# Padded rows for the split down weights, and later free times in the list of TensorE's work

## Chip, core and metric

The kernel runs as one program on 1 core of a Trainium2 chip. The metric is the device time of one execution in microseconds (us). TensorE (PE) multiplies, VectorE (DVE), ScalarE (ACT) and GpSimd (POOL) work on what it leaves in PSUM, and SyncE (SP) issues most DMAs.

## What is computed

```python
xn = layernorm(x)                      # x: 1 x 2048 x 576, float32
q, k, v = split(xn @ wqkv)             # 32 heads of 18 columns
p = softmax(q @ k.T * 18 ** -0.5)      # per head, 2048 x 2048
s = heads(p @ v) @ wo
g = silu(((xn @ w_gate) * (xn @ w_up)) @ w_down)   # 4608 inner columns, no bias
return x + s * g
```

All operands are float32. The kernel keeps the accuracy by splitting each operand into a high part (rounded to the format that TensorE reads at one pass) and a low part (the rest), and sums three products of parts.

## The kernel before

**Stages.** A first part (to about 193 us) normalizes x, makes the columns of x, q, k and v, and splits weights. A middle part computes the 32 heads and the whole gated feed-forward together. A last part (from about 2501 us) multiplies by wo and by the gate.

**Two halves of the array.** In the middle part nearly all matmuls use 64 rows of the array, and two run at once, one on each half (row 0 and row 64). PE takes its instructions in one queue, in the order in which the program lists them. That order is worked out while the program is built, by `order()`: it keeps a clock for each half (`clk[0]`, `clk[1]`), always serves the half that is behind, and picks an item whose inputs and PSUM bank it counts as free. Nothing of this runs on the chip: there only the order remains, and semaphores hold an instruction back where the order was too early.

**The items.** Scores for the row maxima (`a_item`, L712, bank `pa`, read by DVE, L714); scores for the exponentials (`b_item`, L764, bank `pb`, read by ACT, L766); gate and up columns (`gu_op`, L815, 27 matmuls of 512 columns in one of four banks `pg`); down (`down_op`, L876, passes of 6 matmuls of 288 columns). A down pass does six on half 0, hands its bank over to half 1 through a semaphore instruction on another engine (`handing`), and does six on half 1 into the same bank. There are 72 units (4 chunks of 512 tokens by 18 pairs of 128 inner columns), each with 8 such passes. A product of the exponentials with v (`pv_group`, L775, called by `visit`) uses the whole array for up to 8 tiles of a head: three visits for each of the first three heads, two for each other one, 67 in all for 512 tiles. `small` and `soon_now` put the work of the other engines into the same list.

**What the list counts.** An item of 512 columns costs `WIDE` 0.2267 us of its half, one of 288 columns `SHORT` 0.1315 us. `engine(eng, start, length)` gives the end of an operation of another engine; the engine is counted as taken for `length - HIDDEN[eng]` only. A bank counts as free `SPARE` (banks a and b) or `SPARE_G` (the four banks of `pg`) after the end of the operation that reads it, and a handed-over bank a fixed time after the end of the semaphore instruction (`handed`):

```python
HIDDEN = {"DVE": 0.085, "ACT": 0.11, "POOL": 0.03}
SPARE, SPARE_G = 0.27, 0.20
banks[tag][slot] = engine("DVE", clk[r] + 0.43, 0.685) + SPARE
handed[n, k // 6] = engine(eng, clk[0] + 0.33, 0.06) + 0.16
```

**Down's weights.** For each unit the tile `wd` (one buffer) holds, in each of 128 partitions, `[j][e][576]` numbers: j of two blocks of 128 inner columns, e high or low part, and 576 output columns, which are read as two halves of 288 (i = 0, 1). A row of 576 takes 2,304 B, so the second half starts 1,152 B behind the first. In the first pass over the 18 column pairs they are split on the chip (`d_get`: ACT L294, POOL L295) and stored to DRAM (`swd`, L302); the 50 later loads (L286) fetch them from there, as does the last one (`wdl`, L236). `d_get` for the next unit is called when the unit's last down pass has been issued, and the load is queued on SP.

**Raw weights of the first part.** `w_load` fetches blocks of wqkv into one of two buffers of the tag `wraw` (L111, L114); `w_split` reads them (ACT L129, POOL L133). The same tag later holds raw gate and up columns (`g_raw`) and sums (`acc2`).

Of the kernel before, what the change touches and what calls it, by code (L numbers as in the profile page):

```python
# [20 lines left out]
FT = mybir.dt.float32  # L21
# [3 lines left out]
OP = mybir.AluOpType  # L25
# [16 lines left out]
def kernel(  # L42
# [36 lines left out]
    sg = dram.tile([S, D], FT, name="sg")  # L79
    swo = dram.tile([128, 10, D], FT, name="swo")  # L80

    turns = [0]

    def bank(tag, bufs, k=None):
        if tag == "g":
# [20 lines left out]

    def w_load(srcs):

        raw = wpool.tile([128, 2, 5, 128], FT, name="wraw", bufs=2)[:, 0:len(srcs)]
        for i, (m, c0) in enumerate(srcs):  # L110
            nc.sync.dma_start(raw[:, i, 0:4, :],  # L111
                              m[0:512, c0:c0 + 128].rearrange("(k p) c -> p k c", p=128))
            for b in (0, 64):
                nc.sync.dma_start(raw[b:b + 64, i, 4, :], m[512:576, c0:c0 + 128])  # L114
        return raw
# [41 lines left out]
        return wpool.tile([128, 18, 128], FR, name="wgu", bufs=2)  # L157

    def d_tile():
        return wpool.tile([128, 2, 2, D], FR, name="wd", bufs=1)  # L160

    chores, later = [], []
    soon, moves, ordering = [], [], []
    HIDDEN = {"DVE": 0.085, "ACT": 0.11, "POOL": 0.03}
    clk, free, split_at = [0.0, 0.0], {"DVE": 0.0, "ACT": 0.0, "POOL": 0.0}, {}

    def chore(all=True):
# [50 lines left out]
    def columns_of(u):  # L220
        c, q = units[u]
        return NF2 - 1 - q if c % 2 else q
# [8 lines left out]
    def g_get(n):  # L231

        if n == 2 * len(units):
            u = n // 2 - 1
            dw[u] = wpool.tile([128, 2, 2, D], FR, name="wdl", tag="wgu", bufs=2)
            nc.sync.dma_start(dw[u].bitcast(FT), swd[columns_of(u)])  # L236
            ddone.add(u)
        if n >= 2 * len(units):
            return
        f = 2 * columns_of(n // 2) + n % 2  # L240
        if n > 1 and n // 2 % NF2 == 0:
            gw[n] = gw[n - 2]
            gdone.add(n)
            return
        w = gw[n] = g_tile()
        if n >= 2 * NF2:
            nc.sync.dma_start(w.bitcast(FT), swg[f])
            gdone.add(n)
            return
        if n not in graw:  # L250
            ready(gdone, n - 2)
            moves_now()
        raw = graw.pop(n)

        def piece(b):
            nc.scalar.activation(w[:, b:b + 3, :], raw[:, b:b + 3, :], AF.Copy)  # L256
            nc.gpsimd.tensor_tensor(w[:, 9 + b:12 + b, :], raw[:, b:b + 3, :], w[:, b:b + 3, :].bitcast(FT),  # L257
                                    op=OP.subtract)

        def end():  # L260
            gdone.add(n)
            split_at["g", n] = free["POOL"] + 0.2

            def keep():
                nc.sync.dma_start(swg[f], w.bitcast(FT))
                g_load(n + 2)

            move(free["POOL"], keep)

        chores.extend([(piece, (b,)) for b in (0, 3, 6)] + [(end, ())])  # L270
# [5 lines left out]
    def d_get(n):  # L276
        if n >= len(units) - 1:
            return
        p = columns_of(n)
        if n and n % NF2 == 0:  # L280
            dw[n] = dw[n - 1]
            ddone.add(n)
            return
        w = dw[n] = d_tile()
        if n >= NF2:
            nc.sync.dma_start(w.bitcast(FT), swd[p])  # L286
            ddone.add(n)
            return
        if n not in draw:
            moves_now()  # L290
        raw = draw.pop(n)

        def big_piece(k):
            nc.scalar.activation(w[:, k, 0, :], raw[:, k], AF.Copy)  # L294
            nc.gpsimd.tensor_tensor(w[:, k, 1, :], raw[:, k], w[:, k, 0, :].bitcast(FT), op=OP.subtract)  # L295

        def end():
            ddone.add(n)
            split_at["d", n] = free["POOL"] + 0.2

            def keep():
                nc.sync.dma_start(swd[p], w.bitcast(FT))  # L302
                d_load(n + 1)

            move(free["POOL"], keep)

        chores.extend([(big_piece, (k,)) for k in range(2)] + [(end, ())])
# [385 lines left out]
    with ExitStack() as mid:  # L693
# [179 lines left out]
        def down_op(r, u, s, i, ps, n, by):  # L873
            own = alone(u, 2 * s + i)
            j, a, e = DTERMS[n]
            op = nc.tensor.matmul(ps[:, 0:HALF], hs[u][half[r], j, a, s * 128:(s + 1) * 128],  # L876
                             dw[u][half[r], j, e, i * HALF:(i + 1) * HALF],
                             start=(own or r == 0) and n == 0, stop=(own or r == 1) and n == len(DTERMS) - 1)
            if not own and r == 0 and n == len(DTERMS) - 1:
                handing[u, s, i] = by.nop()  # L880
                after(handing[u, s, i], op)
            if not own and r == 1 and n == 0:
                after(op, handing.pop((u, s, i)))
# [202 lines left out]
        slots, gone = {}, [0.0, 0.0]  # L1086
        banks = {"a": [0.0] * 2, "b": [0.0] * 2, "g": [0.0] * 4}
        turn = {"a": 0, "b": 0}
        SPARE, SPARE_G = 0.27, 0.20

        def next_free(tag):
            if tag == "g":
# [236 lines left out]
        def order():  # L1329
# [5 lines left out]
            while going(0) or going(1) or na < TOTAL or nb < TOTAL or due or jobs or soon or pool_later:  # L1335
# [33 lines left out]
                elif op is not None:  # L1369
# [10 lines left out]
                        handed.pop((n, k // 6), None)  # L1380
                    own = kind == "d" and alone(n, k // 6)
                    if kind == "d" and r == 0 and k % 6 == 5 and not own:
                        handed[n, k // 6] = engine(eng, clk[0] + 0.33, 0.06) + 0.16
                        kept[n, k // 6] = slots[0, kind]
                    if end:
                        if kind == "d":
# [136 lines left out]
```

## Time and profile before

| what | value |
|---|---|
| median of 3 runs | 2568.65 us (2568.43 to 2568.83) |
| the profiled execution | 2568.51 us |
| its span, first to last instruction | 2566.7 us |
| PE matmul busy in the span | 2556.5 us |
| DVE, ACT, POOL busy | 1801.8, 1550.5, 682.4 us |
| granted clock of TensorE | 1.00 of full speed |
| DMA queues, time of their packets | 55% of 16 engines' span |

Matmuls are pipelined: the record of one begins before that of its forerunner on the same half has ended, so the engine can read as busy throughout and still lose time. What one costs is the distance from its start to the start of the next on the same half. A row of the timeline joins instructions of one kind that follow each other, and gives the start of the first, the time to the end of the last, and their number; brackets give the idle time of the engine before it, and what ended it.

### The profile page before, as it was taken

The page shows a single profiled execution, that of the slowest core. Times are in us where ns is not written, and L with a number is a line of the kernel's source. Part 1 is how long each engine was busy: PE and PEld are TensorE (multiplying, and loading weights), DVE is VectorE, ACT ScalarE, POOL GpSimd, SP SyncE. Part 2 cuts the span into 40 slices and gives each one's busy share as a digit, 9 for nine tenths or more (in the row PEclk, how much of TensorE's full clock was granted, in tenths as well). Part 3 has the DMA queues.
Part 4 walks back from the last instruction along what each step waited for, and adds up shares of the span by engine and source line. Part 5 has one row for each costly group of instructions (what it writes and reads, how often), then busy time and mean ns, then how long its engine had stood idle before and what let it go on. Part 6 is the DMA issues. An engine that isn't in the chain of part 4 may idle for free.

```text
span 2566.7 us, 59619 instructions
## 1 busy us (share of the span) xinstructions
PE 2556.5 (100%) x24439; PEld 2109.0 (82%) x24439; DVE 1801.8 (70%) x2995; ACT 1550.5 (60%) x3093; POOL 682.4 (27%) x705
## 2 busy tenths in 40 slices
PE   9999999999999999999999999999999999999999
PEld 8899877887887888877788878888788788877789
DVE  6208777777777777777677777777777777777438
ACT  4223677666766656665666656766665666666532
POOL 3214444434421222121211112222211222222016
PEclk9999999999999999999999999999999999999999
DMA  7899767676654345455454445443453453433348
GB/s 234 264 299 261 206 179 193 190 201 193 181 181 136 134 161 159 147 156 166 156 178 130 141 140 165 138 137 137 142 164 107 165 169 129 144 130 125 122 161 268
DMA packets 186641, 435.65 MB, mean 170 GB/s; under 512 B 51104, under 2 KB 112192, under 8 KB 156160
## 3 DMA queue, kind: packets, MB, share of 16 engines
q1 hardware_dynamic: 184208, 423.88, 53.6%
q0 software_dynamic: 2160, 7.96, 0.8%
q8 instruction: 192, 3.15, 0.5%
q14 instruction: 81, 0.66, 0.1%
HBM read 315.16 MB, written 111.35 MB: 166 GB/s over the span
## 4 chain that ended last, share of the span: by engine, by line
PE 98%; DVE 1%; ACT 0%; DMA 0%; issue 0%; SPq 0%; ACTq 0%; DVEq 0%
PE pg L815 36%; PE pg L775 18%; PE pg L876 16%; PE pa L712 11%; PE pb L764 8%; PE pb L493 2%; PE pa L493 2%; PE pg L556 2%; PE pg L1472 1%; PE pa L1472 1%; PE pb L1472 1%; DMA xin<-in_A_x_dram 0%; PE pg L402 0%; PE pa L764 0%; DVE mx L714 0%; PE pb L712 0%
## 5 line engine op out<-in xcount | busy, mean ns | idle before, releaser
L714 DVE TENSOR_REDUCE mx<-pa 128x1 f32<-128x512 f32 x2016 | 1337.3, 686 | 344.9 <-PE pb L764 158.6
L766 ACT ACTIVATE pt<-pb 128x512 f32<-128x512 f32 x2007 | 1149.5, 602 | 478.7 <-PE pb L764 390.5
L815 PE MATMUL pg<-xc,wgu 64*128 64x512 f32 x7776 | 1370.1, 388 | 0.0
L815 PEld LDWEIGHTS pg<-xc,wgu 64*128 64x128 f32 x7776 | 1034.7, 184 | 50.1
L876 PE MATMUL pg<-wd,hs 64*128 64x288 f32 x6816 | 843.2, 293 | 0.0
L876 PEld LDWEIGHTS pg<-wd,hs 64*128 64x128 f32 x6816 | 784.4, 184 | 11.1 <-issue 0.8
L712 PE MATMUL pa<-whole,turning 64*128 64x512 f32 x1999 | 773.7, 394 | 0.5 <-DVE mx L714 0.3
L764 PE MATMUL pb<-whole,turning 64*128 64x512 f32 x1984 | 769.1, 394 | 0.5 <-ACT pt L766 0.3
L775 PE MATMUL pg<-pt,vt 128*32 128x512 f32 x4096 | 453.4, 594 | 0.0
L856 POOL TENSOR_TENSOR hs<-us,hs 128x512 fp32r<-128x512 f32 x144 | 185.8, 1290 | 922.0 <-ACT hs L840 696.8
L712 PEld LDWEIGHTS pa<-whole,turning 64*128 64x128 f32 x1999 | 362.9, 184 | 69.5 <-issue 53.8
L764 PEld LDWEIGHTS pb<-whole,turning 64*128 64x128 f32 x1984 | 360.2, 184 | 6.8 <-ACT pt L766 1.2
L775 PEld LDWEIGHTS pg<-pt,vt 128*32 128x32 f32 x4096 | 126.3, 110 | 284.8 <-issue 280.7
L903 POOL TENSOR_TENSOR acc<-acc,st 128x288 f32<-128x288 f32 x285 | 230.0, 809 | 486.7 <-ACT st L933 303.3
L781 DVE TENSOR_TENSOR oc<-oc,pg 128x512 f32<-128x512 f32 x35 | 24.1, 688 | 219.9 <-PE pg L775 206.4
L257 POOL TENSOR_TENSOR wgu<-wraw,wgu 128x384 fp32r<-128x384 f32 x108 | 108.3, 1016 | 211.7 <-ACT wgu L256 139.9
L779 ACT ACTIVATE oc<-pg 128x512 f32<-128x512 f32 x32 | 19.1, 598 | 229.0 <-PE pg L775 211.1
L939 DVE TENSOR_TENSOR acc<-acc,pg 128x288 f32<-128x288 f32 x260 | 116.0, 448 | 32.5 <-PE pg L876 28.4
L933 ACT ACTIVATE st<-pg 128x288 f32<-128x288 f32 x285 | 118.1, 414 | 25.4 <-PE pg L876 19.3
L832 DVE TENSOR_TENSOR us<-pg,us 128x512 f32<-128x512 f32 x144 | 98.5, 684 | 37.4 <-PE pg L815 22.6
L825 ACT ACTIVATE us<-pg 128x512 f32<-128x512 f32 x143 | 85.5, 598 | 62.6 <-PE pg L815 57.2
L840 ACT ACTIVATE hs<-us 128x512 fp32r<-128x512 f32 x142 | 89.4, 629 | 14.1 <-DVE us L832 14.0
(166 smaller groups left out, 1291.6 us busy)
## 6 DMA issues: line engine op xcount, KB each, us to landing
wgu<-swg SPq DMA_DIRECT2D x102, 1152.0 KB
wd<-swd SPq DMA_DIRECT2D x50, 1152.0 KB
swg<-wgu SPq DMA_DIRECT2D x36, 1152.0 KB
whole<-sqk SPq DMA_DIRECT2D x192, 144.0 KB
turning<-sqk SPq DMA_DIRECT2D x384, 72.0 KB
swd<-wd SPq DMA_DIRECT2D x18, 1152.0 KB
sqk<-hl SPq DMA_DIRECT2D x32, 512.0 KB
xc<-sx SPq DMA_DIRECT2D x24, 512.0 KB
```

The lines of the kernel that those rows point to most:

```text
L257: nc.gpsimd.tensor_tensor(w[:, 9 + b:12 + b, :], raw[:, b:b + 3, :], w[:, b:b + 3, :].bitcast(FT), op=OP.subtract)
L712: nc.tensor.matmul(p, q[rows, t * 128:(t + 1) * 128], k[rows, c * 512:(c + 1) * 512], start=True, stop=True)
L714: nc.vector.tensor_reduce(mx[h][:, t, c:c + 1], p, axis=AX.X, op=OP.max)
L764: nc.tensor.matmul(p, k[rows, t * 128:(t + 1) * 128], q[rows, c * 512:(c + 1) * 512], start=True, stop=True)
L766: nc.scalar.activation(pt[t, c // 2][:, c % 2, :], p, AF.Exp, scale=scale)
L775: nc.tensor.matmul(p[32 * c:32 * c + 32, :], vt[h // 2][:, t, 6 * (h % 2):6 * (h % 2) + 32], pt[t, c // 2][:, c % 2, :], start=t == ts[0], ...
L815: nc.tensor.matmul(ps, gw[n][half[r], a, :], xg[i][half[r], e, :], start=k == 0, stop=k == len(TERMS) - 1)
L856: nc.gpsimd.tensor_tensor(hj[:, 1, :], h32, hj[:, 0, :].bitcast(FT), op=OP.subtract)
L876: op = nc.tensor.matmul(ps[:, 0:HALF], hs[u][half[r], j, a, s * 128:(s + 1) * 128], dw[u][half[r], j, e, i * HALF:(i + 1) * HALF], start=( ...
L903: nc.gpsimd.tensor_tensor(a, a, st, op=OP.add)
L933: nc.scalar.activation(st, ps[:, 0:HALF], AF.Copy)
L939: nc.vector.tensor_tensor(a, a, ps[:, 0:HALF], op=OP.add)
```

## The change

Three things change together.

1. The tile of down's split weights gets rows of 2 x 320 numbers of which 2 x 288 are used, so that the second half starts 1,280 B behind the first, and the tile takes 10,240 B of each partition in place of 9,216 B. Stores, loads, the split and the matmuls address the used part. In DRAM nothing changes; a load or store now has eight pieces of 1,152 B for each partition in place of one of 9,216 B. The last unit's tile (`wdl`) keeps its packing.
2. To make room, `w_load` uses the two halves of one tile of 10,240 B that shares the buffer of `wd`, and the two `wraw` buffers become 4,608 B each in place of 5,120 B.
3. The list counts more: DVE is taken 0.008 us and ACT 0.006 us longer for each operation, banks a and b come free 0.10 us later, those of `pg` 0.08 us later, and a handed-over bank 0.08 us later.

```diff
     def w_load(srcs):
-        raw = wpool.tile([128, 2, 5, 128], FT, name="wraw", bufs=2)[:, 0:len(srcs)]
+        if not raw_pair:
+            raw_pair.append(wpool.tile([128, 2, 2, 5, 128], FT, name="wpair", tag="wd", bufs=1))
+        raw = raw_pair[0][:, turns[1] % 2, 0:len(srcs)]
+        turns[1] += 1
...
     def d_tile():
-        return wpool.tile([128, 2, 2, D], FR, name="wd", bufs=1)
+        return wpool.tile([128, 2, 2, 2, 320], FR, name="wd", bufs=1)
+
+    def d_part(w):
+        return w[:, :, :, :, 0:HALF]
+
+    def d_stored(p):
+        return swd[p].rearrange("p j e (i d) -> p j e i d", i=2)
...
-    HIDDEN = {"DVE": 0.085, "ACT": 0.11, "POOL": 0.03}
+    HIDDEN = {"DVE": 0.077, "ACT": 0.104, "POOL": 0.03}
...
-            nc.sync.dma_start(w.bitcast(FT), swd[p])
+            nc.sync.dma_start(d_part(w.bitcast(FT)), d_stored(p))
...
         def big_piece(k):
-            nc.scalar.activation(w[:, k, 0, :], raw[:, k], AF.Copy)
-            nc.gpsimd.tensor_tensor(w[:, k, 1, :], raw[:, k], w[:, k, 0, :].bitcast(FT), op=OP.subtract)
+            src = raw[:, k].rearrange("p (i d) -> p i d", i=2)
+            nc.scalar.activation(w[:, k, 0, :, 0:HALF], src, AF.Copy)
+            nc.gpsimd.tensor_tensor(w[:, k, 1, :, 0:HALF], src, w[:, k, 0, :, 0:HALF].bitcast(FT), op=OP.subtract)
...
-                nc.sync.dma_start(swd[p], w.bitcast(FT))
+                nc.sync.dma_start(d_stored(p), d_part(w.bitcast(FT)))
...
-                             dw[u][half[r], j, e, i * HALF:(i + 1) * HALF],
+                             dw[u][half[r], j, e, i, 0:HALF],
...
-        SPARE, SPARE_G = 0.27, 0.20
+        SPARE, SPARE_G = 0.37, 0.28
...
-                        handed[n, k // 6] = engine(eng, clk[0] + 0.33, 0.06) + 0.16
+                        handed[n, k // 6] = engine(eng, clk[0] + 0.33, 0.06) + 0.24
```

## Rows read from the trace of the kernel before

**Rows 1.** The page: each engine's busy us, share of the span, instructions.

```profile
PE 2556.5 (100%) x24439; PEld 2109.0 (82%) x24439; DVE 1801.8 (70%) x2995; ACT 1550.5 (60%) x3093; POOL 682.4 (27%) x705
```

**Rows 2.** Windows: stretch, its us, busy PE, PEld, DVE, ACT, POOL; clock, DMA share, GB/s.

```profile
193.50:2501.20 2307.70, 2306.27 (x22945) 1882.18 (x22945) 1678.24 (x2760) 1474.19 (x2922) 594.58 (x600) 1.00 0.52 159
```

**Rows 3.** Lines by form: count, busy us, mean ns, idle before; matmuls of the middle part.

```profile
L815 PE MATMUL pg<-xc,wgu 64*128 64x512 f32 x7776 | 1370.1, 388 | 0.0
...
L876 PE MATMUL pg<-wd,hs 64*128 64x288 f32 x6816 | 843.2, 293 | 0.0
L712 PE MATMUL pa<-whole,turning 64*128 64x512 f32 x1999 | 773.7, 394 | 0.5 <-DVE mx L714 0.3
L764 PE MATMUL pb<-whole,turning 64*128 64x512 f32 x1984 | 769.1, 394 | 0.5 <-ACT pt L766 0.3
```

**Rows 4.** Timeline of PE in the first part (start, us, instruction, forms, count).

```profile
62.86 7.63 PE L556 MATMUL pg<-wv,xcx 128*128 128x288 f32 x56
70.33 3.12 PE L493 MATMUL pb<-xc,wgu 128*128 128x512 f32 x13
73.28 0.39 PE L493 MATMUL pb<-xc,ninth 128*128 128x512 f32 x1
```

**Rows 5.** Timeline of PE, last part: the first group of three repeats, the next repeat.

```profile
2509.47 3.88 PE L1472 MATMUL pa<-wos,oT 128*128 128x288 f32 x28
...
2554.03 3.88 PE L1472 MATMUL pa<-wos,oT 128*128 128x288 f32 x28
```

**Rows 6.** Timeline of PE at the end of one visit of eight tiles.

```profile
1026.01 7.07 PE L775 MATMUL pg<-pt,vt 128*32 128x512 f32 x64
1033.01 0.50 PE L712 MATMUL pa<-whole,turning 64*128 64x512 f32 x1
...
1033.35 0.39 PE L712 MATMUL pa<-whole,turning 64*128 64x512 f32 x1
```

**Rows 7.** Each line's own view: count, then duration min/median/max in ns.

```profile
L815 PE MATMUL pg<-xc,wgu x7776: 383/386/502, 193.7 to 2477.9; 64*128 64x512 f32 x200
...
L876 PE MATMUL pg<-wd,hs x6816: 285/292/403, 215.7 to 2493.9; 64*128 64x288 f32 x195
...
L712 PE MATMUL pa<-whole,turning x1999: 383/386/502, 193.4 to 2396.3; 64*128 64x512 f32 x200
...
L764 PE MATMUL pb<-whole,turning x1984: 383/387/502, 245.7 to 2479.2; 64*128 64x512 f32 x199
```

**Rows 8.** Timeline of PE at 1224 us: two scores that start late.

```profile
1224.26 0.49 PE L712 MATMUL pa<-whole,turning 64*128 64x512 f32 x1 [0.27 <-DVE mx L714]
...
1225.23 0.50 PE L712 MATMUL pa<-whole,turning 64*128 64x512 f32 x1
```

**Rows 9.** Timeline of DVE in the same stretch.

```profile
1224.49 1.96 DVE L714 TENSOR_REDUCE mx<-pa 128x1 f32<-128x512 f32 x3
```

**Rows 10.** DMA in 2374.5:2379, one load of wd: packets, MB, share of 16 engines.

```profile
q1 hardware_dynamic: 143, 1.18, 70.8%
```

**Rows 11.** DMA in 38:44, mostly packets under 2 KB.

```profile
q1 hardware_dynamic: 1172, 1.66, 87.5%
```

**Rows 12.** Timeline of SP: a tight load of wd, and the load of rows 10.

```profile
1889.08 0.34 SPq L286 DMA_DIRECT2D wd<-swd  x1
...
2373.97 0.34 SPq L286 DMA_DIRECT2D wd<-swd  x1
```

**Rows 13.** Timeline of PE: the first use of the tight load.

```profile
1895.90 0.29 PE L876 MATMUL pg<-wd,hs 64*128 64x288 f32 x1
```

**Rows 14.** Tile vt: issue time in ns of its loads, 16 pieces for each partition.

```profile
L699 SPq DMA_DIRECT2D vt<-sv x16: 376/388/938, 201.9 to 2232.8; - x16
```

**Rows 15.** Tile wraw: an issue of 512 pieces on SP, and the first part's splits.

```profile
L147 SPq DMA_DIRECT2D wraw<-in_B_w_gate_dram x36: 638/1424/2777, 113.3 to 686.2; - x36
...
L129 ACT ACTIVATE wgu<-wraw x12: 297/466/634, 15.7 to 106.2; 128x512 fp32r<-128x512 f32 x6, 128x128 fp32r<-128x128 f32 x6
```

**Rows 16.** Tile wd: ACT's half of the split, duration, first and last start.

```profile
L294 ACT ACTIVATE wd<-draw x36: 668/680/714, 163.3 to 759.8; 128x576 fp32r<-128x576 f32 x36
```

More of the change, by code (lines that the diff above doesn't have):

```diff
@@ L80 @@
     swo = dram.tile([128, 10, D], FT, name="swo")
-    turns = [0]
+    turns = [0, 0]
+    raw_pair = []
     def bank(tag, bufs, k=None):
@@ L234, in g_get @@
             u = n // 2 - 1
-            dw[u] = wpool.tile([128, 2, 2, D], FR, name="wdl", tag="wgu", bufs=2)
-            nc.sync.dma_start(dw[u].bitcast(FT), swd[columns_of(u)])
+            dw[u] = wpool.tile([128, 2, 2, 2, HALF], FR, name="wdl", tag="wgu", bufs=2)
+            nc.sync.dma_start(dw[u].bitcast(FT), d_stored(columns_of(u)))
             ddone.add(u)
```

## The prediction

> **What bounds the kernel now.** I read the page first. TensorE is busy 2556.5 us, 100% of the span, and the others at most 70% [rows 1], so only a shorter TensorE list can shorten the kernel. Then I asked whether "busy" means "at full rate", since records overlap. In the middle stretch, 2307.7 us long and with PE busy throughout [rows 2], I set the work against its own pace. An item of 512 columns takes (73.28 - 70.33) / 13 = 226.9 ns from start to start [rows 4]. One of 288 columns takes (2554.03 - 2509.47) / 336 = 132.6 ns (three repeats of 28 + 28 + 56, whose first row and the one behind the third stand there) [rows 5]. A tile of a visit takes (1033.01 - 1026.01) / 8 = 0.875 us [rows 6]. By the loops there are 7,776 gate and up items, 2 x 2,048 scores and 6,912 down items, and two run at once: 11,872 / 2 x 0.2269 = 1346.9 us, 6,912 / 2 x 0.1326 = 458.3 us, and 512 tiles give 448.0 us. Together 2253.2 us, so 54.5 us of the stretch is lost though PE reads as busy.
>
> Part of that is no wait. After a visit the first pair of items takes 1033.35 - 1033.01 = 0.34 us in place of 0.227 [rows 6]: 67 visits x 0.11 = 7.4 us. The change of stage ahead of a visit and the 32 small turns of the row maxima are not priced by a row; I allow 0 to 0.2 us for each of 99, up to 20 us. So 27 to 47 us remain for items that start late or halves that run dry.
>
> A second view agrees in size. A late start shows in the item's own duration: 502 against a median of 386 ns for scores, 403 against 292 for down [rows 7], some 0.11 us. Two such scores stand in the timeline, 0.49 and 0.50 us long, the first after 0.27 us of idle that a DVE reduction ended [rows 8]. Mean less median, times the count, adds up all late starts: 8 x 1,999 (L712), 7 x 1,984 (L764), 2 x 7,776 (L815) and 1 x 6,816 (L876) [rows 3, 7] give 16.0 + 13.9 + 15.6 + 6.8 = 52.3 us over both halves. Less 67 x 2 x 0.11 = 14.7 us behind visits it is 37.6, or 19 us of the span. The means are rounded to 1 ns, so this is good to some 5 us. I take 20 us as what late hand-overs and banks cost.
>
> **Padding.** The same 288-column matmul can be compared at both starts. A run of 56 that only reads second halves, 1,152 B behind a row's start, takes (70.33 - 62.86) / 56 = 133.4 ns each [rows 4]. A run with as many first as second halves takes 132.6 [rows 5], so first halves take 131.8. The difference is 1.6 ns. That is v and wo at 128 rows, not down at 64; I carry it over, since down's second half has the same offset. The padded second half is a whole 1,280 B on, and I take it to behave as the first does. Half of 6,912 less the last unit's 48 (unpadded), over two halves of the array, is about 1,700 items in a row: 1,700 x 1.6 ns = **2.7 us less**; bounds 0 and, by the rounding of the rows, 4.
>
> What the Trainium skill says speaks against this: SBUF — State Buffer, section "Door 1: The DMA port swizzle", puts the cost of an access at crossings of 16-byte lines. Both 1,152 and 1,280 are multiples of 16, so by it padding would be worth nothing and the sum would be 2.7 us higher; the rows above disagree with that, and no run here shows the padded tile yet.
>
> **Transfers of wd.** 50 loads and 18 stores go out in 1,152-B pieces. One load alone in a stretch of 4.5 us moved 1.18 MB in 70.8% of 16 engines [rows 10], 23.1 B/ns on each engine, or 3.19 us. A stretch that is mostly small packets moved 1.66 MB in 87.5% of 6 us [rows 11], 19.8 B/ns, or 3.72 us. So a transfer takes about 0.5 us longer. The issue on SP took 0.34 us [rows 12]; sixteen pieces for each partition took 0.39 [rows 14], 512 pieces on another pattern 1.42 [rows 15], so an issue costs 0.05 to 1.1 us more, and I take 0.05, since eight pieces lie nearer to the first. What queues behind it on SP (loads of gate and up columns, of the stacks for q and k) shifts by that. The tightest load that I found was issued at 1889.08 and first used at 1895.90 [rows 12, 13], 6.8 us later. The load issued at 2373.97 moved all its bytes before 2379 [rows 10, 12], so one takes at most 5.1 us from issue to landing, and 1.7 us are spare; 0.5 + 1.1 us still fit. So nothing on PE waits: 0 us. If that cover were gone, each load as tight would cost what it is late, some 0.5 us.
>
> The split of wd on ACT and POOL writes the same count of numbers (0.68 us on ACT [rows 16]); a second dimension may cost it some hundredths, at most 36 times, beside PE: 0. The pair of raw buffers alternates as the two did. Its last reader on ACT starts at 106.2 us [rows 15], the first write of wd in its buffer comes at 163.3 [rows 16], so 57 us cover it: 0. Were a half to wait for the other's load, the first part would lose a load's time once or twice, at most 5 us.
>
> **The list.** No operation is added. Items that need a bank are placed up to 0.10 us (a, b), 0.08 us (pg) or, for a pass on half 1, 0.08 us later, and other ready items come before them. A semaphore that came up to 0.1 us too late for an item then comes in time; the loss that goes with it is the 0.11 us above. The second score of [rows 8] is such a case: it starts at 1225.23, right behind the end of the reduction that began at 1224.49 (with the kernel's own 0.685 us, 1225.18) [rows 8, 9]. The first score of [rows 8], 0.27 us late, is cured only in part. The longer counts for DVE go the right way too: three reductions in a row stand (1.96 - 0.685) / 2 = 0.64 us apart [rows 9], where the old count is 0.600 and the new one 0.608. Bounds: 0, and the whole 20 us. I take a third, **7 us less**, because part of the lateness is larger than 0.1 us, because items that are put off bring others forward which may be early in their turn, and because some of the lateness has causes that no margin of the list touches (a long chain on DVE).
>
> Sum on the profiled execution: 2568.5 - 2.7 - 7 = 2558.8 us; the median before differs by 0.1 us, which I leave out.
>
> **Rivals.** First, the list only changes where it stalls: each new order has as many early items as the old one, since their cause is the scatter of DVE and ACT. For it: the three reductions stand 0.64 us apart where even the new count says 0.608 [rows 9]. Against it: margins of 0.1 us are as large as the usual lateness. It gives 2568.5 - 2.7 = 2565.8 us, or 2563.5 to 2571 with a little either way.
>
> Second, the padding does nothing and the list works: 2568.5 - 7 = 2561.5 us. For it: no row times down's own halves apart. Against it: 336 and 56 items on two other lines differ by the offset alone. The rule of the Trainium skill's page SBUF — State Buffer named above would have it so.
>
> Third, slower: the four banks of pg run short. A gate and an up item hold one each for 27 items, and a down pass holds one over both halves. Its life in the list grows by 0.08 + 0.08 us; it is now about 6 x 0.13 + 0.55 + 6 x 0.13 + 0.2 + 0.45 + 0.2 = 3.0 us (the kernel's own counts), so 5% more. Where no bank is left, a half gets nothing while the other goes on, and on the chip it runs dry. If every one of 576 passes lost 0.16 us on one half, that were 46 us of the span; the gain of 9.7 us is gone at one pass in five, and at one in three it is 2568.5 + 5.6 = 2574 us. Against it: scores need no bank of pg and fill a half at any time.
>
> **How the numbers follow.** 0.2% is 5.1 us, about what a measurement of this kernel tells from no change. The forecast, padding and list both working (2549 to 2563), has 0.60. The first rival has 0.20, the second 0.06, the third 0.14. Faster: 0.60 + 0.06 = 0.66; same: 0.20; slower: 0.14. The range goes from 2549 (padding 2.7 and most of the 20 us) to 2571, which takes in the first rival and leaves out most of the third.
>
> **What would show it.** Right: down's own view keeps its median, but runs of 288 columns get nearer to 131.8 ns; the middle stretch is about 10 us shorter with PE as busy; the means of L712 and L764 fall from 394 towards 390. The loads of wd issue in about 0.4 us and no PE item waits for them. Wrong: means that stay at 394 or rise while L815's rises too (the list moved its stalls), a middle stretch with idle gaps ended by wd's loads, or a first part longer than 193 us.

## The result, and the profile after

| what | before | after |
|---|---|---|
| median, runs taken side by side on one chip | 2568.54 us (2567.84 to 2569.30) | 2580.09 us (2578.20 to 2581.18) |
| ratio, 95% interval | | 1.0044 (1.0034 to 1.0055) |
| profiled execution, its span | 2568.51, 2566.7 us | 2581.18, 2579.0 us |
| first score starts | 193.4 us | 193.6 us |
| from there to the start of the last down matmul ("middle") | 2307.5 us | 2310.0 us |
| from there to the end ("end") | 65.8 us | 75.5 us |

The changed kernel is slower by 11.5 us, 0.44%. The forecast was 2558.8 us, faster; its range ended at 2571. The last three lines of the table are start times of matmuls in the trace; they say at once that 9.7 of the 12.3 us of span are lost in the last part, where the change edits nothing.

The page after (busy us, share, instructions) answers to [rows 1]:

```profile
PE 2561.0 (99%) x24439; PEld 2117.6 (82%) x24439; DVE 1795.0 (70%) x2963; ACT 1563.3 (61%) x3125; POOL 708.5 (27%) x737
```

Windows of the changed kernel, columns as in [rows 2], first the middle and the end, then four short stretches:

```profile
193.50:2503.60 2310.10, 2307.16 (x22945) 1887.54 (x22944) 1668.77 (x2722) 1485.36 (x2950) 620.48 (x632) 1.00 0.53 158
2503.60:2579.00 75.40, 63.57 (x451) 62.78 (x449) 58.31 (x91) 15.58 (x35) 40.71 (x49) 0.92 0.78 253
...
240.00:247.00 7.00, 7.00 (x60) 5.61 (x56) 4.07 (x7) 2.21 (x7) 4.20 (x4) 1.00 0.98 295
248.60:255.30 6.70, 6.58 (x42) 6.44 (x44) 3.39 (x5) 4.49 (x10) 1.14 (x2) 0.50 0.65 168
2496.00:2503.60 7.60, 7.60 (x84) 4.37 (x76) 2.96 (x6) 0.00 (x0) 0.00 (x0) 1.00 0.00 0
2508.30:2518.30 10.00, 7.55 (x30) 7.24 (x31) 3.71 (x8) 3.25 (x8) 0.00 (x0) 0.50 0.96 295
```

The last part of the kernel before, the same columns:

```profile
2501.20:2566.70 65.50, 59.86 (x448) 59.40 (x448) 56.09 (x85) 13.79 (x31) 40.45 (x49) 1.00 0.83 269
```

PE is busy for 63.57 of the last 75.40 us, so 11.8 us there are idle, 6.2 more than the 5.6 of the kernel before. And in two stretches with work TensorE was granted half its clock, 1.2 GHz: for 6.7 us from 248.6, and for 10 us from 2508.3. Ahead of each it had the full clock and was busy throughout (7.00 of 7.00, 7.60 of 7.60 us). What happened between is told by the waits of PE (total us, times, longest):

```profile
PE pg L1483 <- ACT oT L1466: 4.9, 1, 4.9
PE pg L1483 <- DMA wos<-swo: 1.9, 1, 1.9
PE pb L775 <- DMA whole<-mr: 1.7, 1, 1.7
```

None of the three is in the trace of before. They belong to two places where one kind of work hands over to the next.

**Change-over one: the first head's exponentials.** The scores for the exponentials need the row maxima of the head, which go through DRAM (`mr`) into the stack (`whole`). The timeline of the changed kernel, PE and then SP:

```profile
246.78 0.29 PE L887 MATMUL pg<-wd,hs 64*128 64x288 f32 x1
248.72 0.76 PE L775 MATMUL pb<-whole,turning 64*128 64x512 f32 x1 [1.65 <-DMA whole<-mr]
```

```profile
238.51 2.95 SPq L333 DMA_DIRECT2D whole<-sqk  x3
241.58 1.23 SPq L761 DMA_DIRECT2D whole<-mr  x2
```

And SP before:

```profile
240.00 1.23 SPq L750 DMA_DIRECT2D whole<-mr  x2
241.32 1.16 SPq L322 DMA_DIRECT2D whole<-sqk  x3
```

The two loads have changed places. In the new order the next head's stack goes out first, and the row maxima that PE waits for are issued 1.6 us later. SP's order is no decision of the chip: `rows` puts the load of the maxima into the list at the time at which the list counts it as due (`move(done, load)`), and with longer counts that time slipped behind the stack's.

**Change-over two: from the last head to the output projection.** Behind the last visit come DVE's division and transposes, the store `sot`, the load `oin`, ACT's `oT`, and only then wo. What hides this chain is the down work that is left. PE, DVE, SP and ACT of the changed kernel:

```profile
2499.78 0.61 PE L786 MATMUL pg<-pt,vt 128*32 128x512 f32 x4
2500.32 3.56 PE L887 MATMUL pg<-wdl,hs 64*128 64x288 f32 x40
2508.80 2.29 PE L1483 MATMUL pg<-wos,oT 128*128 128x288 f32 x8 [4.93 <-ACT oT L1466]
2513.03 3.22 PE L1483 MATMUL pg<-wos,oT 128*128 128x288 f32 x12 [1.94 <-DMA wos<-swo]
...
2500.53 0.69 DVE L792 TENSOR_TENSOR oc<-oc,pg 128x512 f32<-128x512 f32 x1 [6.89 <-PE pg L786]
...
2503.70 1.37 SPq L806 DMA_DIRECT2D sot<-oc  x4
2505.18 0.39 SPq L1438 DMA_DIRECT2D oin<-sot  x1
...
2508.65 0.58 SPq L1034 DMA_DIRECT2D wos<-swo  x1
...
2508.12 0.63 ACT L1466 ACTIVATE oT<-oin 128x512 fp32r<-128x512 f32 x1 [13.21 <-DMA oin<-sot]
```

From the visit's end at about 2500.3 to the first wo matmul are 8.5 us; 40 down matmuls cover 3.56 of them. In the kernel before, the timeline of PE shows the last visit 11 us earlier, with 148 down matmuls behind it:

```profile
2482.19 7.07 PE L775 MATMUL pg<-pt,vt 128*32 128x512 f32 x64
2489.19 3.29 PE L876 MATMUL pg<-wd,hs 64*128 64x288 f32 x43
...
2497.87 3.32 PE L876 MATMUL pg<-wdl,hs 64*128 64x288 f32 x35 [0.40 <-DVE acc L939]
2501.11 0.80 PE L1472 MATMUL pg<-wos,oT 128*128 128x288 f32 x4
```

There wo follows with no wait. The new list leaves less down work for the end.

The grouped lines of the middle part stand as before in [rows 3]:

```profile
L826 PE MATMUL pg<-xc,wgu 64*128 64x512 f32 x7776 | 1361.9, 388 | 0.2 <-DMA wgu<-swg 0.2
L887 PE MATMUL pg<-wd,hs 64*128 64x288 f32 x6816 | 823.9, 293 | 0.9 <-DVE acc L950 0.7 <-DMA wd<-swd 0.2
L723 PE MATMUL pa<-whole,turning 64*128 64x512 f32 x1999 | 772.9, 394 | 0.2 <-DVE mx L725 0.2
L775 PE MATMUL pb<-whole,turning 64*128 64x512 f32 x1977 | 766.3, 395 | 1.7 <-DMA whole<-mr 1.7
```

The means of the two scores, which the forecast wanted to see fall from 394 towards 390, are 394 and 395.

### The profile page after: what moved, and what is told of

It is laid out like the page before. It is cut to its first block, busy times and chain, and to the rows that moved or that the text cites. A ratio compares the mean times of both kernels' runs of the same rounds, so it can differ in the third digit from the quotient of the medians.

```text
span 2579.0 us, 59699 instructions
## 1 busy us (share of the span) xinstructions
PE 2561.0 (99%) x24439; PEld 2117.6 (82%) x24439; DVE 1795.0 (70%) x2963; ACT 1563.3 (61%) x3125; POOL 708.5 (27%) x737
## 4 chain that ended last, share of the span: by engine, by line
PE 97%; DMA 1%; DVE 1%; SPq 0%; issue 0%; ACT 0%; DVEq 0%; ACTq 0%
PE pg L826 35%; PE pg L786 17%; PE pg L887 16%; PE pa L723 11%; PE pb L775 8%; PE pb L504 2%; PE pa L504 2%; PE pg L567 2%; PE pg L1483 1%; PE pa L1483 1%; PE pb L1483 1%; DMA wgu<-swg 0%; PE pa L775 0%; DMA xin<-in_A_x_dram 0%; DMA whole<-mr 0%; DVE mx L725 0%
## 5 line engine op out<-in xcount | busy, mean ns | idle before, releaser
L826 PEld LDWEIGHTS pg<-xc,wgu 64*128 64x128 f32 x7776 | 1047.0, 184 | 48.4 <-ACT st L944 0.5
L887 PE MATMUL pg<-wd,hs 64*128 64x288 f32 x6816 | 823.9, 293 | 0.9 <-DVE acc L950 0.7
L887 PEld LDWEIGHTS pg<-wd,hs 64*128 64x128 f32 x6816 | 767.8, 185 | 12.2 <-DVE acc L950 1.0
L914 POOL TENSOR_TENSOR acc<-acc,st 128x288 f32<-128x288 f32 x317 | 255.8, 809 | 559.0 <-ACT st L944 305.7
L944 ACT ACTIVATE st<-pg 128x288 f32<-128x288 f32 x317 | 130.6, 413 | 17.8 <-PE pg L887 7.0
L950 DVE TENSOR_TENSOR acc<-acc,pg 128x288 f32<-128x288 f32 x228 | 101.6, 447 | 35.1 <-PE pg L887 21.8
```

Of the source, the lines that this page charges most:

```text
L826: nc.tensor.matmul(ps, gw[n][half[r], a, :], xg[i][half[r], e, :], start=k == 0, stop=k == len(TERMS) - 1)
L914: nc.gpsimd.tensor_tensor(a, a, st, op=OP.add)
L944: nc.scalar.activation(st, ps[:, 0:HALF], AF.Copy)
```

## The experiments

All times are medians beside runs of the kernel before on the same chip. "Middle" and "end" are the two stretches of the table above, in the profiled execution. "Late" counts, from the trace, the matmuls of the four kinds of the middle part whose record is more than 60 ns longer than the median of their line. Margins are a/b (old 0.27 us), pg (0.20), hand-over (0.16) and the two counts (DVE 0.085, ACT 0.110).

| run | differs from before by | middle | end | late | median | ratio (95%) |
|---|---|---|---|---|---|---|
| before | | 2307.5 | 65.8 | 378 | 2568.5 | 1 |
| after | padding, all new margins | 2310.0 | 75.5 | 407 | 2580.1 | 1.0044 (1.0034, 1.0055) |
| e1 | padding alone | 2306.9 | 66.0 | 384 | 2568.5 | 1.0001 (0.9992, 1.0010) |
| e2 | all margins, no padding | 2309.0 | 76.1 | 382 | 2577.8 | 1.0039 (1.0026, 1.0053) |
| e3 | after, row maxima loaded first | 2305.2 | 75.9 | 374 | 2576.3 | 1.0031 (1.0019, 1.0043) |
| e4 | e3, last visit earlier | 2307.0 | 65.1 | 354 | 2566.8 | 0.9994 (0.9985, 1.0003) |
| e5 | padding, a/b 0.37 | 2304.9 | 69.4 | 351 | 2568.8 | 1.0001 (0.9991, 1.0011) |
| e6 | padding, hand-over 0.24 | 2316.4 | 64.8 | 442 | 2576.4 | 1.0032 (1.0020, 1.0043) |
| e7 | after, 84 unread matmuls ahead of wo | 2307.4 | 75.9 | 389 | 2578.7 | 1.0039 (1.0024, 1.0054) |
| e8 | e1, second halves of down at 256 columns, part of the output left out | 2292.1 | 66.9 | | 2555.2 | 0.9949 (0.9934, 0.9964) |
| e9 | e5, last visit earlier | 2304.6 | 66.2 | 343 | 2566.0 | 0.9990 (0.9982, 0.9999) |
| e10 | padding, pg 0.28 | 2307.1 | 66.6 | 400 | 2568.7 | 1.0001 (0.9992, 1.0010) |
| e11 | padding, counts 0.077, 0.104 | 2317.8 | 67.3 | 445 | 2580.5 | 1.0047 (1.0033, 1.0061) |
| e12 | e9, pg 0.28 | 2307.0 | 65.7 | 357 | 2567.4 | 0.9996 (0.9987, 1.0005) |
| e13 | padding, a/b 0.275 | 2311.8 | 64.8 | 402 | 2573.3 | 1.0019 (1.0010, 1.0028) |
| e14 | padding, hand-over 0.17 | 2308.5 | 64.8 | 395 | 2568.2 | 0.9999 (0.9990, 1.0008) |
| e15 | padding, counts 0.084, 0.109 | 2319.0 | 66.4 | 453 | 2580.4 | 1.0047 (1.0031, 1.0064) |
| e16 | padding, hand-over 0.25 | 2313.6 | 64.8 | 426 | 2573.2 | 1.0020 (1.0011, 1.0030) |
| e17 | e9, counts 0.084, 0.109 | 2306.6 | 65.6 | 352 | 2563.9 | 0.9985 (0.9975, 0.9994) |
| e18 | e9, hand-over 0.17 | 2307.3 | 64.8 | 367 | 2566.9 | 0.9994 (0.9985, 1.0004) |

Two limits of this table. First, a single trace scatters: after, e2 and e7 issue the same list up to the last part and have the same wait for the first row maxima, and their middles are 2310.0, 2309.0 and 2307.4 us. So a difference of 2 or 3 us between two middles decides nothing by itself. Second, "late" also counts matmuls that ran at half the clock: 42 in after, 23 each in e2 and e7, 37 in e11, 21 in e14, 28 in e15, 45 in e17, none in the others. Without them after has 365, no more than the kernel before.

**e1 and e2: the two parts of the change apart.** e1 has after's tile with the old numbers of the list, e2 the old tile with the new numbers.

> The padded tile, the pieces of 1,152 B and the shared buffer alone, with the old counts of the list, so the order of TensorE's work is the old one. Theory A (the loss of the changed kernel sits at two change-overs that the new order disturbs, the padding itself gains): 2565.8 us, 2.7 less than before, and the median distance between down's items falls only where second halves are read. Rival B (the padding gains nothing): 2568.5. Rival C (the 1,152-B pieces of the transfers hold back TensorE or SP, and that is the loss): above 2571, up to 2580.

> The new counts of the list alone, with the old tile and transfers. Theory A: the two change-overs are lost just as in the changed kernel and the padding's gain is missing, 2582.8 us, with a wait of about 1.7 us at 247 us and one of about 5 us near 2504 us, each followed by the halved clock. Rival B: 2580.1, as the changed kernel. Rival C: 2568 or less, without the waits.

The list alone brings the loss (e2: 9.7 of the 11.5 us, with the same waits at both change-overs), and the padding alone nothing that can be told from zero (e1). e2 came out below both of its forecasts for a loss; its interval and that of after overlap, so the 1.8 us between the two aren't told apart.

**e3 and e4: the two change-overs, one after the other.** e3 orders the load of the first head's row maxima 2 us earlier in the list; TensorE's order stays that of after. e4 adds that, once only the last head's scores for the exponentials are left to place, none of them is put off to a planned time any more; 188 down matmuls then stand behind the last visit.

```diff
-            move(done, load)
+            move(done - 2.0 if job[2] == 0 else done, load)
...
                 if nb >= TOTAL - N:
-                    goal = clk[r] + lean
+                    goal = 0.0
```

> The changed kernel, with one edit: the load of the first head's row maxima is put into SP's queue ahead of the next head's stack, as it stood before; TensorE's order is the changed kernel's. Theory A: the wait of 1.65 us near 247 us and the 6.8 us of halved clock behind it go, 2580.1 - 1.65 - 3.4 = 2575 us. Rival (the drop of the clock has another cause, and the wait is only in its place): the wait goes and the clock still drops there, 2578.4.

> The changed kernel with the edit of the start and one more: in the last head the scores go first, ahead of gate, up and down items, so that 188 down items in place of 40 lie behind the last visit. Theory A: the wait of 4.9 us and that of 1.9 us near 2504 us and the 10.2 us of halved clock go too, 2575 - 9.6 = 2565.5 us, so that the new margins as such neither gain nor lose. Rival D (the new margins lose in the bulk of the middle part): above 2569. Rival E (they gain there, as I forecast): 2559.

The granted clock of e3 in the stretch of change-over one, and PE of e4 at change-over two:

```profile
248.60:255.30 6.70, 6.66 (x83) 6.20 (x82) 5.69 (x11) 6.31 (x14) 4.10 (x4) 1.00 0.64 167
```

```profile
2479.71 5.33 PE L786 MATMUL pg<-pt,vt 128*32 128x512 f32 x48
...
2486.13 5.68 PE L887 MATMUL pg<-wd,hs 64*128 64x288 f32 x74
...
2496.91 3.19 PE L887 MATMUL pg<-wdl,hs 64*128 64x288 f32 x34 [0.34 <-DVE acc L950]
2500.03 0.80 PE L1483 MATMUL pg<-wos,oT 128*128 128x288 f32 x4
2501.70 1.58 PE L1483 MATMUL pg<-wos,oT 128*128 128x288 f32 x10 [0.86 <-DVE oT L1468]
```

The first edit gives back 3.8 us (2580.1 to 2576.3), the second 9.5 (2576.3 to 2566.8), 13.3 together where 11.5 had been lost. In e3 the stretch that did 42 matmuls at half clock does 83 at full clock; its middle is 4.8 us shorter than that of after, of which 1.65 was the wait, and 2.2 us shorter than that of e7, which has the same wait and only 3.4 us at half clock behind it. So the loss of the change is these two stalls, shown by undoing each. With them mended, all the margins and the padding together, which were to bring 9.7 us, stand 0.06% from the kernel before, inside the interval.

**e7: what of the end is clock.** 84 unread matmuls of 128 columns keep TensorE busy between down and wo.

> The changed kernel with 84 matmuls of 128 columns, which no one reads, between the last down item and the first item of the last part, some 4.8 us in the wait of 4.9 us. Theory A, of which the clock is a part: the wait stays as long, but the clock no longer halves behind it, so of 10.2 us at half speed about 5 us come back: 2575 us. Rival (the wait alone is the loss, the clock is in its shadow): 2580.

PE of e7, then windows: behind its wait for the first row maxima, its filled stretch, and wo behind that:

```profile
2497.14 3.56 PE L887 MATMUL pg<-wdl,hs 64*128 64x288 f32 x40
2500.62 9.60 PE L1474 MATMUL pa<-identr 128*128 128x128 f32 x84
2510.05 3.13 PE L1486 MATMUL pg<-wos,oT 128*128 128x288 f32 x22
```

```profile
249.30:252.70 3.40, 3.40 (x25) 3.30 (x25) 2.10 (x4) 2.15 (x6) 1.00 (x1) 0.50 0.84 176
...
2500.60:2510.00 9.40, 9.40 (x85) 9.38 (x85) 3.29 (x8) 1.66 (x4) 0.00 (x0) 1.00 0.65 185
2510.00:2520.40 10.40, 10.40 (x80) 10.40 (x80) 6.37 (x11) 2.49 (x6) 2.35 (x3) 1.00 1.03 333
```

The filler took 9.5 us, about twice what I had meant, so wo began later than it could have, and the total moved only 1.4 us, to a time between the two forecasts. But the parts can be told: from the first wo matmul to the end are 2576.3 - 2510.1 = 66.2 us with the clock kept and no wait for `wos`, against 2579.0 - 2508.8 = 70.2 in after. So the second wait (1.94 us) and the halved clock cost 4.0 us together, which leaves some 2.1 for the clock, by difference only, and the delay of the first wo matmul (5.2 us behind the start of the last down matmul in place of 0.2) is the largest piece, 5.0.

**e5, e6, e10, e11: one margin at a time**, each with the padding. In the expectations up to e7, theory A is that the loss sits at the change-overs. From e9 on, theory A is that each margin has a worth of its own and these add up, and theory B that each new order is a draw, whatever its margins.

> The padded tile with one of the new counts alone: banks a and b free 0.10 us later. In this order 100 down items lie behind the last visit, where the kernel before has 148 and the changed one 40; the load of the first row maxima stands ahead of the next stack, as before. Theory A (what follows the last visit decides): from the end of the last visit to the first item of the last part the changed kernel needed 8.5 us; 100 items cover 100 / 2 x 0.132 = 6.6 us, so TensorE stands still about 2 us near 2500 us, and nothing at 247 us: 2568.5 + 2 = 2570.5 us if the clock stays up, 2575 if it halves. Rival E (a margin for a and b saves late starts in the bulk): below 2565.

> The padded tile with another of the new counts alone: the handed-over bank 0.08 us later. In this order 266 down and some 100 gate and up items lie behind the last score or visit, and the first load stands as before. Theory A: no wait at either change-over, so 2568.5 us within 3, plus what the feed-forward alone at the end loses because no score fills in. Rival D (each margin loses time in the bulk): above 2572 without a wait at a change-over.

> Padding and the pg margin of 0.28 us alone; 148 down items behind the last visit, the row maxima loaded ahead of the stacks, so neither change-over should stall. The hand-over margin alone cost 9.5 us of the middle stretch, the a/b margin alone gained 2.0, all together with both change-overs mended gave 2307.0 against 2306.9 with padding alone. Theory A (the margins' worths add up): the pg margin and the longer counts share -7.5 us between them; with half of it here 2568.5 - 3.7 = 2565 us. Theory B (they don't add up, each order is its own draw): anywhere from 2563 to 2576 us, with no relation to the sum. Rival: banks of pg run short, as the prediction's third rival says; then the first matmuls of gate and up items start late more often and the middle is longer by over 3 us.

> Padding and the two engine counts alone (0.077 and 0.104 us of fixed time in place of 0.085 and 0.11); 136 down items behind the last visit. Theory A (worths add up): the rest of the -7.5 us, so that this middle stretch and the one of the pg margin, each against 2306.9 us, together give about -7.5. Theory B: no such sum; both may come out longer than 2306.9. Without a trend, 2568.5 us, 3 either way.

Against e1's middle of 2306.9 they give -2.0 (a/b), +9.5 (hand-over), +0.2 (pg) and +10.9 us (counts, 4.0 of it a wait for the row maxima as in after): +18.6 in all, where the four together give +0.1 (e4). The worths don't add up. e5 has 100 down matmuls behind the last visit, and its end is 3.4 us longer than that of e1. e6 has no stall at a change-over and loses all the same, in the bulk, as its rival D had it, with 442 late matmuls against 384.

**e9 and e12: the a/b margin with the end mended, and pg added.**

> Padding, the a/b margin of 0.37 us, and the last visit put earlier, so that 158 down items stand behind it in place of 100. The run with that margin alone had a middle stretch of 2304.9 us, 2.0 less than with padding alone, and lost it at the end (69.4 us behind the last down item begins, in place of 66.0, with waits of 1.06 and 1.19 us). Theory A (each margin has a worth of its own in the bulk, and the end only needs enough down work behind the last visit): no wait at the output projection, clock 1.0 there, the tail back at about 65.8 us, and 2568.8 - 3.6 = 2565 us. Theory B (a new order of the list is a new draw of late starts, several us up or down, whatever its margins): the middle stretch moves by more than 2 us as the end of the list changes little, or the gain of 2.0 isn't there, and the time is at 2568 or above.

> Padding, the a/b margin of 0.37 and the pg margin of 0.28 us together with the last visit put earlier (192 down items and 33 of gate and up behind the last score). Theory A: middle stretch = 2306.9 - 2.0 + what the pg margin alone gives, within 1.5 us, and no wait at the end; about 2561 to 2566 us. Theory B: it misses that sum by 3 us or more.

e9 repeats the middle of e5 (2304.6 against 2304.9; the two lists agree up to the last head, so it is the same draw once more) and loses nothing at the end. e12 misses the sum of its parts (2305.1) by 1.9 us: between what the two theories said, so it decides nothing by itself.

**e13 to e16: margins changed by 1 to 10 ns.** A late semaphore of 100 ns can't be cured by 5. But each of these edits re-orders the list of TensorE from the first heads on.

> Padding, and the a/b margin changed by 5 ns only (0.275 us in place of 0.27): too little to make any late semaphore come in time, but it re-orders the list from the first exponentials on. 196 down items stand behind the last visit and the row maxima are loaded ahead of the stacks, so no change-over should stall. Theory A (a margin's size sets the bulk): the middle stretch stays at 2306.9 us within 1 us, 2568.5 us. Theory B (each order is a draw of its own): the middle moves by 2 us or more, up or down, with the number of late starts.

> Padding, and the hand-over changed by 10 ns only (0.17 us in place of 0.16); 192 down items behind the last visit, row maxima first. Theory A: a worth in proportion to the 9.5 us that 80 ns cost, so 1.2 us longer, 2569.7 us. Theory B: the middle differs from 2306.9 us by 2 us or more either way, or not at all, with no proportion to the 10 ns.

> Padding, and the two engine counts changed by 1 ns each (0.084 and 0.109 us). 148 down items behind the last visit, but SP loads the first head's row maxima behind the next head's three stack loads. Theory of the change-over: TensorE waits for the row maxima at about 247 us, 1.6 to 4 us, and the granted clock falls to 0.5 behind it, though no margin is changed to speak of; 2 to 5 us longer for that, at the end no wait. For the bulk from 300 us on: theory A, as with padding alone within 1 us; theory B, off by 2 us or more.

> Padding, and a hand-over of 0.25 us in place of the 0.24 that made the middle stretch 2316.4 us; 207 down items behind the last visit, row maxima first. Theory A (a longer hand-over is slow by itself): 2316 to 2318 us again, 2576 to 2578 us in all. Theory B (that order was a bad draw): the middle comes back by 3 us or more, 2573 us or less.

5 ns on the a/b margin cost 4.9 us of the middle and 1 ns on the counts 12.1 (1.6 of it the wait for the first row maxima), where theory A allowed 1 us. The other two decide nothing. 10 ns on the hand-over cost 1.6 us, near the 1.2 of theory A, but the trace also holds a wait of 2.2 us for the row maxima of a later head; and a hand-over of 0.25 us is 2.8 us shorter in the middle than one of 0.24, between the two theories. With e13 and e15 no proportion is left: theory A falls, and what remains is that each order is a draw. e15 shows change-over one with the old margins all but untouched; SP and the lines of PE:

```profile
238.05 2.95 SPq L333 DMA_DIRECT2D whole<-sqk  x3
241.12 1.23 SPq L761 DMA_DIRECT2D whole<-mr  x2
```

```profile
L887 PE MATMUL pg<-wd,hs 64*128 64x288 f32 x6816 | 855.2, 293 | 1.7 <-DMA wd<-swd 1.6
L723 PE MATMUL pa<-whole,turning 64*128 64x512 f32 x1999 | 776.3, 395 | 0.7 <-DVE mx L725 0.7
L775 PE MATMUL pb<-whole,turning 64*128 64x512 f32 x1981 | 770.4, 396 | 1.6 <-DMA whole<-mr 1.6
```

The means of the scores are 1 to 2 ns above those of [rows 3], and 453 matmuls are late. So that stall is no property of the new margins: a change of 1 ns can bring it.

**e17 and e18: the same small changes with the wide a/b margin.** Is the a/b margin just another draw, or does it make draws better?

> The a/b margin of 0.37 us with padding and the earlier last visit (166 down items behind it), and on top of it the same 1 ns on the two engine counts that took padding alone from 2568.5 to 2580.4 us and its middle stretch from 2306.9 to 2319.0. Theory B (every order is a plain draw, whatever the margin): the middle lies anywhere in the 2306.9 to 2319.0 of the eight orders with the old a/b margin, most likely 2309 or longer. Theory C (the wider a/b margin makes orders good on average, and the kernel before is a lucky order of the old margin): the middle is 2304.5 to 2307.5 as in the three orders with 0.37 us so far, plus about 1.6 us if TensorE waits for the row maxima at 247 us, which here again are loaded behind the three stacks; 2565.5 to 2570 us in all.

> The a/b margin of 0.37 us with padding and the earlier last visit (185 down items behind it), and the hand-over changed by 10 ns. Theory B: a middle stretch anywhere from 2306.9 to 2319.0 us, most likely 2309 or longer. Theory C: 2304.5 to 2307.5 us, no wait at either change-over, 2565 to 2568.5 us in all.

Both stay low: 2306.6 and 2307.3. The profiled execution of e17 has two waits for row maxima in it, the longer one of 3.02 us, with the clock at half behind it (timeline, then windows of PE ahead of it and behind it):

```profile
1888.22 0.50 PE L723 MATMUL pa<-whole,turning 64*128 64x512 f32 x1
1891.74 0.69 PE L775 MATMUL pb<-whole,turning 64*128 64x512 f32 x1 [3.02 <-DMA whole<-mr]
```

```profile
1880.00:1888.00 8.00, 8.00 (x75) 2.98 (x72) 0.79 (x2) 0.61 (x3) 1.29 (x1) 1.00 0.97 353
1891.80:1895.20 3.40, 3.40 (x20) 3.33 (x22) 0.69 (x1) 1.51 (x4) 0.00 (x0) 0.50 0.00 0
```

That execution took 2567.63 us, the longest of ten; the median is 2563.91. Only it has a trace, so that the others lack the wait of 3.02 us is likely, not shown. Theory C had it at 2565.5 to 2570. e17 is the fastest version tried that computes all of the output, 0.15% (0.06 to 0.25) ahead of the kernel before and some 0.6% ahead of the changed one.

Five orders with the wide margin and the end mended (e4, e9, e12, e17, e18) have middles of 2304.6 to 2307.3 us, mean 2306.5. Eight orders with a/b at 0.27 or 0.275 (e1, e6, e10, e11, e13 to e16) have 2306.9 to 2319.0, mean 2312.6. The kernel before, whose order e1 shares, stands at the low end of the eight. The numbers of late matmuls go with this, 343 to 367 against 384 to 453 (307 to 367 against 374 to 442 without those at half clock), and over all runs but e8 the middle by and large rises with that number. Stalls don't make the difference: waits for row maxima take 1.1 us of an order in the five, as a mean, and 1.0 in the eight. Nor, as far as two pairs can tell, does the earlier last visit, which the five have and the eight lack: e9 with it is like e5 without, and e4 with it is not shorter than e3 (2307.0 against 2305.2).

**e8: what a matmul's time is worth.** The second halves of down, but for the first matmul of each pass, are cut from 288 to 256 columns.

> The padded tile with the old counts (the kernel of the padding alone) and the old order; in second halves the down items but the first of each pass multiply 256 in place of 288 columns, so part of the output is left out. That shortens 1,440 items on one half of the array and 1,728 on the other by 13.3 ns, 21 us as the mean of the halves, where the padding shortened some 1,700 by 1.6 ns. If time saved in down's items passes on in full: 2568.5 - 21 = 2547 us, and the padding's 2.7 us must have been lost elsewhere (transfers, first part). If the order holds it back, because what waits for other engines comes at the same times: well above 2547, 2558 at half.

By that estimate 21 us of matmul time in a row were taken away, and the kernel became 13.3 us shorter against before: 63% passes through. That the rest is taken up by what the halves wait for is likely, not shown; its trace has a wait of 1.5 us for `wd`, where that of e1 has one of 0.3.

## Why the prediction was wrong

**The step that failed is the list, "7 us less".** It failed in two ways. First, it priced the margins only where the list stalls all along the middle, and took everything else that the list decides as given. Two such things changed: the place of one load in SP's queue, and how much down work is left behind the last visit. The prediction did ask what is queued on SP, but only behind the loads of `wd`, and of one tightest load; it never followed `move(done, load)`, whose due time comes from the counts that were changed. And it never asked what covers the chain from the last visit to wo, which the trace of before shows with 148 matmuls ahead of it. e3 and e4 put 3.8 and 9.5 us on these, 13.3 of the 21.3 us between forecast and result. The other 8.0 are what e4 (2566.8) still lacks of the forecast.

Second, it took the order before as a typical one. The gain of wider margins over a typical order of the old margin may well be real: the means of five and eight orders differ by 6.1 us, near the 7 forecast. But the kernel before isn't typical, its order is one of the best of its kind, and a change of the list throws that draw away. So against this kernel the margins gave nothing in the middle (e4 2307.0, e1 2306.9, both padded) in place of 7. That the wide a/b margin makes draws better rests on five against eight orders, and on orders that differ in other margins too; it is supported, not settled. Why the hand-over of 0.24 and the counts do badly with the old a/b margin, and not with the new one, stays open.

**Padding, "2.7 us less".** Its local part held. Start to start on one half of the array, the second halves of down took 133.3 to 133.6 ns in the kernel before and 131.4 to 132.0 in e1 and after (medians, on either half, of passes of six that nothing breaks, from all starts in the traces), so the 1.6 ns carried over from [rows 4, 5], from 128 rows to 64, were right. The size in the kernel was not: at e8's 63%, 2.7 us become 1.7, and e1's interval reaches from 2.1 us less to 2.6 us more. Between 0 and 2.1 us the gain can't be told. The rule of the Trainium skill's page SBUF — State Buffer, section "Door 1: The DMA port swizzle", that an access pays where it crosses to a new 16-byte line, would have had the two starts alike; the 1.6 ns of the matmuls disagree with it, the time of the kernel doesn't say.

**Transfers of wd.** The packets, their share of the queues, and the issues on SP (min/median/max), before and then in e1, which has the same list:

```profile
q1 hardware_dynamic: 184208, 423.88, 53.6%
...
L286 SPq DMA_DIRECT2D wd<-swd x50: 320/343/2264, 827.9 to 2466.1; - x50
```

```profile
q1 hardware_dynamic: 245136, 423.88, 55.8%
...
L296 SPq DMA_DIRECT2D wd<-swd x50: 529/584/1973, 827.7 to 2465.6; - x50
```

An issue costs 0.24 us more, not the 0.05 that I took, within the bound of 1.1. The same bytes take 2.2 points more of the queues' time; over the span of 2566 us and 68 transfers that is some 0.8 us for each, an estimate, where I took 0.5. "PE waits for nothing" nearly held: 0.2 us in after, but 1.6 us in e15, so that cover was thin. The split on ACT took 687 ns in place of 680 at the median (677 in e1), and the first part ended at 193.6 in place of 193.4 us: both at nothing, as forecast.

**The rivals.** The first, that the list only changes where it stalls (2565.8 us), had the right idea of the bulk, with far too narrow a spread: eight orders spread over 12 us. It saw no change-over. The third had the sign, and the wrong mechanism: the pg margin alone (e10) costs 0.2 us in the middle, and the range left the measured time out. The chance of slower, 0.14, was too low: in the trace of before PE waits only once at the two change-overs, for 0.6 us inside wo, so a new order could hardly gain there and could lose.

## What to carry to other kernels

Where a list is worked out ahead and counted in tenths of a microsecond, an edit of its numbers is a new draw of the whole order: compare a nudge of a few nanoseconds beside it before calling a gain or a loss the edit's own. Ahead of such an edit, look at the hand-overs between stages first: for each, which load goes ahead of which in the queue, and how many us of other work cover the chain; here some hundred short matmuls fewer there cost 9.5 us, more than the 7 that were hoped for in the bulk. And a margin is to be judged by several orders with it and without it, not against the one order that is in use.

## What was not expected of the hardware

- The granted clock fell to half behind short waits of a TensorE that had been busy at full clock: 1.65 us of waiting, then 0.50 in the 6.7 us from 248.6 (after); the same wait in e7, then 0.50 for 3.4 us; 3.02 us, then 0.50 for 3.4 us (e17). The price is only what TensorE would have done in that time: in after 42 matmuls in place of 83, about 3.2 us of the 4.8.
- 84 matmuls of 128 x 128 by 128 columns took 9.60 us, 114 ns each, close to the 131.8 ns of one with 288 columns.
- From e9 to e15 the middle grows by 14.4 us with 110 more late matmuls, though two halves of the array share the work. Of the 14.4, 1.6 us is e15's wait for row maxima, 1.6 are its waits for `wd`, and 3.4 us of it ran at half clock, which holds 28 of the late ones. With half of these 3.4 us taken off too, about 0.12 us are left for each of the other 82, an estimate.
